# Turned k copied into k's place with a head's rows side by side, and 48 of 64 columns in the k-v product

## The chip, the core and the metric

The kernel runs on one core of a Trainium2 chip, as one launch. The metric is the device time of that launch in microseconds, the median of several runs. The core's engines run side by side: TensorE (PE, matrix products into the PSUM banks; PEld is its loading of weights), VectorE (DVE), ScalarE (ACT), GpSimd (POOL) and SyncE (SP), which issues nearly all DMAs here.

## The reference

A gated linear attention over 768 steps, for 4 batches and 8 heads of 48 columns, and then two dense blocks. In float32 throughout:

```python
for t in range(S):
    state = alpha[:, :, t, :, None] * state + np.einsum('bhd,bhe->bhde', k[:, :, t], v[:, :, t])
    y[:, :, t] = np.einsum('bhd,bhde->bhe', q[:, :, t], state)
x = y.transpose(0, 2, 1, 3).reshape(B * S, H * D)          # 3072 x 384
h = np.maximum(x @ w_in, 0.0); x = h * h @ w_out            # 384 -> 2048 -> 384
h = x @ w_in2;  out = (h / (1.0 + np.exp(-1.702 * h))) @ w_out2
```

## The kernel before

The attention is done in chunks of 64 steps. A step n = 0 to 23 of the kernel handles half of the batches of one chunk (8 pairs of 128 partitions). For each n, `load` brings q, k, decays (tile `raw`, two buffers) and v; `decays`, `ratios`, `carry` prepare them on DVE; `scores`, `state`, `intra` and `gain` are small products on PE; `before`, `causal`, `leave`, `update` move their results on ACT and DVE. `gain(n)` is the k-v product that `update(n)` adds to the state S; it needs k with the steps on the partitions, that is, turned.

The dense blocks work on 512 tokens at a time, with 16 slices j of the hidden width. `inner` (line 182) makes a slice h in one PSUM bank of a rotation of five (`ps`; the banks Y of `scores` and X of `intra` are of the same rotation), ACT takes it out by a relu (L192) and squares it (L197), DVE splits it into a high and a low part (L201, L208), and `outer` (L223) multiplies it on, one or two j later. Every 4 j of the first dense layer form a block m, in which one step of the attention is done as well: `group(m)` holds `scores(m+1)`, `state(m+1)`, `intra(m)`, `gain(m)`, the work on their results, `load(m+2)` and the turning of y and k. In a block with m = 8, 12, 16, 20 the group stands at the fourth j (a late group), in the others at the third. The products of PE in a group other than a late one are followed by the `inner` of the fourth j, in a late one by an `outer`. In the blocks m = 9 to 21 the next layer's weights are also brought in (`w_load`, L79), and made into floats (`w_abs` on ACT, L87, then L96, L99, L102 on DVE). The order of the code is the order on each engine.

For n up to 8, k is turned by PE (`turn`) and copied back into its own place by ACT (`turned`, L432). From n = 9 on, `k_turn` does it without PE: DVE transposes 32 x 32 squares (L455), SP writes them to DRAM in four pieces (L446, tensor `dram_k`), and reads them back turned (L450) into `turned_k`, of which there are two. y goes the same way ahead of k (`y_squares`, L463, `dram_y`), except for m = 11, 15, 19, 23, where PE turns it. The y that came back is split by `x_hi` (L145, ACT) and `x_lo` (DVE) at the second j of the next block.

Of the kernel before, what the change touches and what calls it, by code (L numbers as in the profile page):

```python
# [12 lines left out]
ALU = mybir.AluOpType  # L13
PSUM = bass.MemoryType.PSUM

B, H, S, D = 4, 8, 768, 48
# [3 lines left out]
NHS = (S // CH) * 2  # L20
# [238 lines left out]
def fast(ctx, tc, qka, vs, wpk, out):  # L259
# [8 lines left out]
    nc = tc.nc  # L268
# [45 lines left out]
    def seg(t):  # L314
        return t.rearrange("p (n s) -> p n s", s=SEG)


    st = {}
# [67 lines left out]
    def quarters():  # L386

        for hp in range(4):
            for s in range(2):
                for w in range(2):  # L390
                    yield hp, s, w, 64 * (1 - w)
# [44 lines left out]
    squares = x2[:, 0, NTOK - 512:], x2[:, 1, NTOK - 512:NTOK - 512 + DM]  # L436
    turned_y = x2[:, 2, NTOK - 512:NTOK - 512 + DM]
    turned_k = x2[:, 0:2, NTOK - 1024:NTOK - 512]
# [3 lines left out]
    def shuffle(dst, src, room):  # L442

        w = src.shape[1] // 4
        for i in range(4):
            nc.sync.dma_start(  # L446
                out=room[:, i * w:(i + 1) * w].rearrange("(g p) c -> p g c", g=4),
                in_=src[32 * i:32 * i + 32].rearrange("p (g c) -> p g c", g=4),
            )
        nc.sync.dma_start(out=dst, in_=room)  # L450

    def k_turn(n):
        if n + 2 < NHS:
            k = st[n]["k"]
            nc.vector.transpose(  # L455
                out=squares[0].rearrange("p (g d h) -> p h g d", g=4, h=4),
                in_=k.rearrange("p (h g d) -> p h g d", g=4, h=4),
            )
            shuffle(turned_k[:, n % 2], squares[0], dram_k)
            st[n]["kt"] = turned_k[:, n % 2].rearrange("p (w d h) -> p w h d", w=2, h=4)  # L460

    def y_squares(n):
        nc.vector.transpose(  # L463
# [26 lines left out]
    def gain(n):  # L490

        s = st[n]
        if n + 2 < NHS:
            for hp, b, w, r in quarters():
                h, p = 2 * hp + w, slice(64 * b, 64 * b + 64)
                k = s["kt"][p, 1 - w, hp] if "kt" in s else s["k"][p, hp * 128 + r:hp * 128 + r + 64]
                nc.tensor.matmul(  # L497
                    s["X"][int(r == 64 * b)][r:r + 64, (4 + hp) * D:(5 + hp) * D],
                    lhsT=k, rhs=s["v"][p, h * D:(h + 1) * D],
                    start=True, stop=True,  # L500
                )

# [5 lines left out]
    def heads(t):  # L508
        return t.rearrange("p (h e) -> p h e", e=D)
# [14 lines left out]
    def update(n):  # L524

        if n + 2 < NHS:
            z = S[n % 2].rearrange("p (h b e) -> p h b e", b=2, e=D)
            for b in range(2):
                u = heads(st[n]["X"][1 - b][:, 4 * D:8 * D])
                if n < 2:  # L530
                    nc.scalar.copy(z[:, :, b, :], u)
                else:
                    nc.vector.tensor_tensor(out=z[:, :, b, :], in0=u, in1=z[:, :, b, :], op=ALU.add)

    def sum_up():
        nc.scalar.activation(out=stats, in_=stats, func=AF.Square, accum_out=total)
# [36 lines left out]
    def fill(n):  # L573
        for _ in range(n):
            nc.tensor.matmul(idle_ps, lhsT=idle[:, 0:128], rhs=idle[:, 128:], start=True, stop=True)
# [15 lines left out]
    def pre_split(bi, m):  # L591
# [4 lines left out]
    doing = dict(  # L596
        load_a=load_a, load_q=load_q, decays=decays, ratios=ratios, swap=swap, carry=carry, measure=measure, scores=scores, state=state,
        before=before, causal=causal, turn=turn, turned=turned, intra=intra, gain=gain, leave=leave, update=update,
        y_turn=y_turn, x_hi=x_hi, x_lo=x_lo, k_turn=k_turn, y_squares=y_squares,
    )  # L600

    def do(n, *fs):
        if n < NHS:
            for f in fs:
                doing[f](n)
# [8 lines left out]
    def first_block(what):  # L614
        f, n = what.split(":")
        (doing.get(f) or dense[f])(int(n))

    with tc.manual_schedule():
        nc.vector.memset(idle, 0.0)
        order = ORDER.split()  # L620
        while "load" in order[0]:
            first_block(order.pop(0))
        make_identity(nc, ident)
        nc.gpsimd.memset(mask, 1.0)
        for p0 in (0, 64):
            nc.gpsimd.affine_select(
                out=mask[p0:p0 + 64], in_=mask[p0:p0 + 64], compare_op=ALU.is_ge, fill=0.0, base=0,
                pattern=[[1, CH]], channel_multiplier=-1,
            )
        nc.gpsimd.memset(ones, 1.0)  # L630
        nc.vector.memset(c1, 0)
        nc.vector.memset(seg(c1[:, 1:])[:, :, CH:], 1)
        nc.vector.memset(c2, 0.0)

        nc.scalar.activation(out=total, in_=ones, func=AF.Abs)
        fill(13)
        for what in order:
            first_block(what)
        net.pend.append((0, 0, NJ - 1, net.to_sbuf(x2[:, :, 0:512])))

        def group(m):
            do(m + 1, "scores", "state")
            do(m, "intra", "gain")
            do(m + 1, "before", "causal")
            do(m, "leave", "update")
            if m < NHS - 2:
                load(m + 2)
            if m - 7 < NJ:
                net.w_load(1, m - 7)
            if m % 4 < 3:  # L650
                do(m, "y_squares")
            do(m + 1, "k_turn")

        def turns(m):
            if m % 4 == 3:
                do(m, "y_turn")
            do(m, "x_hi", "x_lo")

        for bi in range(1, NB):
            last = bi == NB - 1  # L660
            between = not last
            for j in range(NJ):
                m, i = 4 * bi + 4 + j // 4, j % 4

                t = 4 * (bi - 1) + j // 4
                if between and i == 2:
                    net.w_bits(1, t)
                net.hidden(0, bi, xs[bi], j)
                if between:
                    if i == 0:  # L670
                        do(m + 1, "decays", "swap")
                        if not t:
                            net.w_load(1, t)
                        if t:
                            net.w_send(1, t - 1, home)
                    elif i == 1:
                        do(m + 1, "ratios", "carry")
                        if j > 1:
                            turns(m - 1)
                        net.w_abs(1, t)  # L680
                    elif i == 2:
                        do(m + 1, "measure")
                    else:
                        net.w_store(1, t, home)

                late = between and j // 4 == 0
                if late and i == 3:
                    group(m)
                if last and j == 0:
                    net.w_send(1, NJ - 1, home)  # L690
                if last and j in (5, 8, 11):
                    pre_split(0, (j - 5) // 3)
                net.pend.append((0, bi, j, net.to_sbuf(x2[:, :, bi * 512:(bi + 1) * 512])))
                if between and j == NJ - 1:
                    net.drain(2)
                    turns(m)
                net.drain(1 if j in (0, NJ - 1) else 2)
                if last and j > 1:
                    net.w_fetch(1, j - 2, home)
                if between and i == 2 and not late:  # L700
                    group(m)
        for bi in range(NB):
            for j in range(NJ):
                net.hidden(1, NB + bi, xs[NB + bi], j)
                if bi + 1 < NB and j in (7, 9, 11):
                    pre_split(bi + 1, (j - 7) // 2)
                if bi == 1 and j == 3:
                    sum_up()

                u = bi * NJ + j - 4  # L710
                c = u // 2
                if u % 2 == 0:
                    if 0 <= c < 2 * NJ:
                        test_load(c)
                    if 0 <= c - 1 < 2 * NJ:
                        test_sum(c - 1)
                elif 0 <= c - 1 < 2 * NJ:
                    test_least(c - 1)
                if bi == 4 and j == 12:
                    counted()  # L720
                if bi == 4 and j == 14:
                    verdict()
                if bi == 5 and j == 4:
                    fine = nc.values_load(flag[0:1, 0:1], min_val=0, max_val=1)
                o = net.to_out(out[bi], x2[:, :, bi * 512:(bi + 1) * 512], bi == NB - 1)
                net.pend.append((1, NB + bi, j, o))
                net.drain(1 if j in (0, NJ - 1) else 2)
                if bi == 0 and j < 2:
                    net.w_fetch(1, NJ - 2 + j, home)
        net.drain(0)  # L730
        return fine
# [159 lines left out]
```

## Time and profile before

| | |
|---|---|
| median of 3 runs | 892.84 us (891.68 to 893.05) |
| the profiled execution, time | 892.36 us |
| its span, first to last instruction | 890.6 us |
| TensorE's granted clock, mean over the span | 0.978 of full |
| busy, PE / DVE / ACT / POOL | 98% / 62% / 48% / 0% of the span |

The profile is of one execution. Its span is what the trace shows; 1.76 us of the measured time lie around it. Matmuls overlap in the pipeline, so how long a group of them takes is read from the start of the group to the start of the next.

### The profile page before, as it was taken

To read this page: it belongs to the slowest core of one execution; us is meant where nothing else is said; L and a number is where in the kernel's file an instruction comes from. 1 tells how busy PE (TensorE), PEld (TensorE's weight loads), DVE (VectorE), ACT (ScalarE), POOL (GpSimd) and SP (SyncE) were. 2 spreads that over 40 slices of the span, in tenths; PEclk is the share of its full clock that TensorE was granted. 3 is DMA by queue.
4 is the path that set the end of the run, shared out by engine and by line. 5 is a ranking of instruction groups with operands and counts; after the bars stand their busy time and mean duration, and the time that the engine had idled before them with its cause. 6 is when DMAs were issued, how large, how long until landed. Compare 5 with 4: busy or idle time off the path is not lost.

```text
span 890.6 us, 15856 instructions
## 1 busy us (share of the span) xinstructions
PE 871.2 (98%) x6487; PEld 718.6 (81%) x6487; DVE 548.1 (62%) x860; ACT 423.3 (48%) x824; POOL 1.4 (0%) x10
## 2 busy tenths in 40 slices
PE   6799999999999999999999999999999999999997
PEld 4688888888888888888888888888888888888885
DVE  8999979768887977975333344444544554433332
ACT  4888764445455444554333343543443444433332
POOL 0000000000000000000000000000000000000000
PEclk6599999999999999999999999999999999999999
DMA  8655216653654655342355423422422432200001
GB/s 330 240 197 177 74 36 198 206 192 121 231 182 141 202 178 189 111 179 90 115 204 182 172 71 107 142 79 99 142 104 74 142 107 71 71 1 4 33 0 40
DMA packets 47009, 116.57 MB, mean 131 GB/s; under 512 B 11216, under 2 KB 22480, under 8 KB 46928
## 3 DMA queue, kind: packets, MB, share of 16 engines
q1 hardware_dynamic: 46784, 115.21, 38.1%
q8 instruction: 53, 0.87, 0.4%
q10 hardware_dynamic: 144, 0.26, 0.1%
q14 instruction: 28, 0.23, 0.1%
HBM read 92.39 MB, written 23.07 MB: 130 GB/s over the span
## 4 chain that ended last, share of the span: by engine, by line
PE 94%; DVE 3%; DMA 1%; issue 1%; ACT 0%; SPq 0%; DVEq 0%
PE h L182 44%; PE acc L223 43%; PE X L497 2%; PE Y L401 2%; PE X L485 1%; PE Y L414 1%; PE kp L427 1%; PE tp L141 0%; DMA x<-qka 0%; DVE raw L341 0%; DMA x<-dram_k 0%; DVE wf L99 0%; DVE M L472 0%; DMA dram_k<-x 0%; DVE y L522 0%
## 5 line engine op out<-in xcount | busy, mean ns | idle before, releaser
L182 PE MATMUL h<-x,w 128*128 128x512 f32 x1728 | 424.7, 391 | 0.0
L182 PEld LDWEIGHTS h<-x,w 128*128 128x128 f32 x1728 | 323.9, 188 | 67.8
L223 PE MATMUL acc<-hi,w 128*128 128x512 f32 x1152 | 298.4, 391 | 0.0
L223 PEld LDWEIGHTS acc<-hi,w 128*128 128x128 f32 x1152 | 214.9, 188 | 44.6
L208 DVE TENSOR_TENSOR lo<-g,hi 128x512 fp32r<-128x512 f32 x192 | 132.9, 692 | 75.3 <-ACT hi L201 67.4
L223 PE MATMUL acc<-lo,w 128*128 128x512 f32 x576 | 165.7, 389 | 0.0
L171 DVE TENSOR_TENSOR g<-h,g 128x512 f32<-128x512 f32 x96 | 66.5, 692 | 152.8 <-ACT g L170 152.8
L170 ACT ACTIVATE g<-h 128x512 f32<-128x512 f32 x96 | 57.5, 599 | 155.8 <-PE h L182 155.4
L192 ACT ACTIVATE g<-h 128x512 f32<-128x512 f32 x96 | 57.4, 598 | 151.4 <-PE h L182 151.0
L223 PEld LDWEIGHTS acc<-lo,w 128*128 128x128 f32 x576 | 108.1, 188 | 22.6
L201 ACT CAST hi<-g 128x512 fp32r<-128x512 f32 x112 | 69.5, 620 | 76.4 <-DVE g L171 76.0
L201 DVE CAST hi<-g 128x512 fp32r<-128x512 f32 x80 | 34.0, 425 | 97.1 <-ACT g L197 97.1
L197 ACT ACTIVATE g<-g 128x512 f32<-128x512 f32 x96 | 60.7, 632 | 2.9
L553 DVE TENSOR_REDUCE ends<-test_f 128x1 f32<-128x768 f32 x32 | 30.3, 948 | 0.0
L549 ACT ACTIVATE test_f<-test 128x768 f32<-128x768 f32 x32 | 29.0, 906 | 0.0
L341 DVE TENSOR_TENSOR_SCAN raw<-raw,c 128x520 f32<-128x520 f32 x20 | 24.7, 1234 | 1.1 <-DMA raw<-qka 1.1
L347 DVE TENSOR_TENSOR_SCAN raw<-raw,c 128x520 f32<-128x520 f32 x20 | 24.9, 1242 | 0.7
L357 DVE TENSOR_TENSOR raw<-raw 128x1024 f32<-128x1024 f32 x20 | 24.4, 1218 | 0.0
L384 ACT ACTIVATE raw<-raw 128x1040 f32<-128x1040 f32 x20 | 21.3, 1065 | 5.5 <-DVE raw L357 5.4
L401 PEld LDWEIGHTS Y<-raw 48*64 48x64 f32 x640 | 12.3, 146 | 11.7 <-issue 6.0
L102 DVE SCALAR_TENSOR_TENSOR wf<-wraw,wf 128x768 int32<-128x768 int32 x22 | 21.1, 958 | 0.8
L99 DVE SCALAR_TENSOR_TENSOR wf<-wraw,wf 128x768 int32<-128x768 int32 x22 | 21.1, 958 | 0.8
(90 smaller groups left out, 513.0 us busy)
## 6 DMA issues: line engine op xcount, KB each, us to landing
test<-wpk SPq DMA_DIRECT2D x32, 768.0 KB, 4.3
wraw<-wpk SPq DMA_DIRECT2D x22, 768.0 KB, 4.7
w<-home SPq DMA_DIRECT2D x16, 768.0 KB, 4.3
raw<-qka SPq DMA_DIRECT2D x20, 512.0 KB, 5.6
x<-wpk SPq DMA_DIRECT2D x10, 768.0 KB, 4.4
home<-whi SPq DMA_DIRECT2D x16, 384.0 KB, 3.6
home<-wf SPq DMA_DIRECT2D x16, 384.0 KB, 4.1
raw<-qka SPq DMA_DIRECT2D x20, 260.5 KB, 4.4
```

The costliest lines, as they stand in the source:

```text
L170: nc.scalar.activation(out=g, in_=h, func=AF.Sigmoid, scale=1.702)
L171: nc.vector.tensor_tensor(out=g, in0=h, in1=g, op=ALU.mult)
L182: self.nc.tensor.matmul(h, lhsT=w[:, a, kk * 128:(kk + 1) * 128], rhs=x[:, b, kk, :], start=(i == 0), stop=(i == 3 * KK - 1),)
L192: self.nc.scalar.activation(out=g, in_=h, func=AF.Relu)
L197: self.nc.scalar.activation(out=g, in_=g, func=AF.Square)
L201: copy(hi, self.h_t[key, j][1])
L208: self.nc.vector.tensor_tensor(out=lo, in0=g, in1=hi.bitcast(F32), op=ALU.subtract)
L223: nc.tensor.matmul(acc[m], lhsT=w[:, a, DM + m * 128:DM + (m + 1) * 128], rhs=g, start=(j == 0 and p == 0), stop=(j == NJ - 1 and p == 2),)
L347: nc.vector.tensor_tensor_scan(out=F, data0=F, data1=c2, initial=0.0, op0=ALU.mult, op1=ALU.add,)
L401: nc.tensor.matmul(s["Y"][w][64 * b:64 * b + 64, hp * CH:(hp + 1) * CH], lhsT=s["k"][r:r + D, c], rhs=s["q"][r:r + D, c], start=True, stop ...
L549: nc.scalar.activation(out=f, in_=high, func=AF.Abs, accum_out=ends[:, c:c + 1])
L553: nc.vector.tensor_reduce(out=ends[:, 2 * NJ + c:2 * NJ + c + 1], in_=tests.pop(c), axis=mybir.AxisListType.X, op=ALU.min)
```

## The change

The squares of k are written with the four heads apart (head, then column) and not interleaved, so that a turned k has 32 columns of a head side by side. A new function `k_place` (line 464 of the new code) copies the turned k on ACT from `turned_k` into the place of k in `raw`, with the 128 values of a head's row in one piece. It is called at the second j of each block, after `ratios` and `carry` of m + 1 and ahead of `turns(m - 1)` (which has `x_hi`, L145) and `w_abs` (L87). `gain` then reads k from `raw` for every n, and for n of 8 and more it loads 48 columns, so that it writes 48 of each 64 rows; `update` therefore works on the two pieces of 48 rows.

```diff
-                out=squares[0].rearrange("p (g d h) -> p h g d", g=4, h=4),
+                out=squares[0].rearrange("p (g h d) -> p h g d", g=4, h=4),
...
-            st[n]["kt"] = turned_k[:, n % 2].rearrange("p (w d h) -> p w h d", w=2, h=4)
+    def k_place(n):
+        if n >= 9 and n + 2 < NHS:
+            nc.scalar.copy(
+                st[n]["k"].rearrange("p (h i d) -> p h i d", h=4, i=4),
+                turned_k[:, n % 2].rearrange("p (i h d) -> p h i d", h=4, i=4),
+            )
...
-                k = s["kt"][p, 1 - w, hp] if "kt" in s else s["k"][p, hp * 128 + r:hp * 128 + r + 64]
+                d = D if n >= 8 else 64
                 nc.tensor.matmul(
-                    s["X"][int(r == 64 * b)][r:r + 64, (4 + hp) * D:(5 + hp) * D],
-                    lhsT=k, rhs=s["v"][p, h * D:(h + 1) * D],
+                    s["X"][int(r == 64 * b)][r:r + d, (4 + hp) * D:(5 + hp) * D],
+                    lhsT=s["k"][p, hp * 128 + r:hp * 128 + r + d], rhs=s["v"][p, h * D:(h + 1) * D],
                     start=True, stop=True,
...
-                else:
-                    nc.vector.tensor_tensor(out=z[:, :, b, :], in0=u, in1=z[:, :, b, :], op=ALU.add)
+                    continue
+                for p in (slice(0, D), slice(64, 64 + D)) if n >= 8 else (slice(0, 128),):
+                    nc.vector.tensor_tensor(out=z[p, :, b, :], in0=u[p], in1=z[p, :, b, :], op=ALU.add)
...
                         do(m + 1, "ratios", "carry")
+                        do(m, "k_place")
                         if j > 1:
                             turns(m - 1)
                         net.w_abs(1, t)
```

On ACT, the second and third j of block 10, before the change: relu and square of the second j, the split of y (L145), the weights' abs (L87), relu and square of the third j, then the sum of magnitudes (L384).

```order
L192 ACTIVATE g_2066<-h_2056 128x512 [waits PE_49]
L197 ACTIVATE g_2066<-g_2066 128x512 [waits Activation_49]
L145 ACTIVATE x_1853,stats_96<-x2_104 128x3x128 [waits DMAHW7_49]
L87 ACTIVATE wf_2077<-wraw_1979 128x768 [waits DMAHW6_49,DMAHW2_49]
L192 ACTIVATE g_2101<-h_2091 128x512 [waits PE_49]
L197 ACTIVATE g_2101<-g_2101 128x512 [waits Activation_49]
```

The same place after the change.

```order
L192 ACTIVATE g_2071<-h_2061 128x512 [waits PE_49]
L197 ACTIVATE g_2071<-g_2071 128x512 [waits Activation_49]
L464 COPY raw_1774<-x2_104 128x512 [waits DMAHW4_49,DMAHW0_49]
L145 ACTIVATE x_1856,stats_96<-x2_104 128x3x128 [waits DMAHW7_49]
L87 ACTIVATE wf_2083<-wraw_1984 128x768 [waits DMAHW6_49,DMAHW2_49]
L192 ACTIVATE g_2107<-h_2097 128x512 [waits PE_49]
L197 ACTIVATE g_2107<-g_2107 128x512 [waits Activation_49]
```

The copy (L464) with its wait for transfers (DMAHW) stands ahead of the split of y, the abs and the relu of the third j.

On SP, the end of block 9's DMAs: the sending of weights (L127, L128), then `load(11)` (L326, L330, L331). Lines with - are before, with + after.

```order
 L127 DMA home<-whi 128x768 [waits Activation_49]
 L128 DMA home<-wf 128x768
-L326 DMA raw<-qka 128x521 [waits DMAHW7_49]
+L326 DMA raw<-qka 128x521 [waits DMAHW7_49,PE_49,Activation_49]
 L330 DMA raw<-qka 128x1024
 L331 DMA v<-vs 128x384
```

The load's first DMA now waits for PE and ACT, which use the k in the buffer that it fills; nothing on SP has changed its place.

On PE, `gain(9)` (L504, L497 before) between the last pass of `intra` and the `inner` of the fourth j (L182), after the change.

```order
L492 MATMUL X_1_1935<-v_1012,M_103 64x48
L504 MATMUL X_0_1934<-v_1012,raw_1011 48x48 [waits Activation_49]
L504 MATMUL X_1_1935<-v_1012,raw_1011 48x48 x2
...
L182 MATMUL h_1998<-x_895,w7_902 128x512 [waits Activation_49]
L182 MATMUL h_1998<-x_895,w7_902 128x512 x8
```

`gain` reads `raw` and waits for ACT (before: `x2`, and for DMAs); the `inner` behind it waits for ACT, as it did before, since its bank is that of the slice five banks earlier in the rotation (h of the third j, then two Y and two X).

## Rows read from the trace of the kernel before

**Rows 1.** Page, parts 1 (busy us, share, instructions) and 4 (chain that ended last).

```profile
PE 871.2 (98%) x6487; PEld 718.6 (81%) x6487; DVE 548.1 (62%) x860; ACT 423.3 (48%) x824; POOL 1.4 (0%) x10
...
PE 94%; DVE 3%; DMA 1%; issue 1%; ACT 0%; SPq 0%; DVEq 0%
```

**Rows 2.** Busy time by window: length, PE, PEld, DVE, ACT, POOL, clock, DMA.

```profile
135.60:390.00 254.40, 254.05 (x2636) 211.46 (x2632) 206.46 (x349) 121.26 (x244) 0.00 (x0) 1.00 0.56 183
```

**Rows 3.** PE by time: start, us, line, output<-inputs, count [idle before <-releaser].

```profile
135.02 0.64 PE L497 MATMUL X<-v,raw 64*64 64x48 f32 x32
135.59 1.66 PE L223 MATMUL acc<-hi,w 128*128 128x512 f32 x6
...
152.07 1.18 PE L497 MATMUL X<-v,x 64*64 64x48 f32 x32 [0.35 <-DMA x<-dram_k]
153.17 2.32 PE L182 MATMUL h<-x,w 128*128 128x512 f32 x9
...
170.67 0.65 PE L485 MATMUL X<-v,M 64*64 64x48 f32 x32
171.14 1.13 PE L497 MATMUL X<-v,x 64*64 64x48 f32 x32
172.20 2.36 PE L182 MATMUL h<-x,w 128*128 128x512 f32 x9
...
191.27 2.36 PE L182 MATMUL h<-x,w 128*128 128x512 f32 x9
...
212.74 1.66 PE L223 MATMUL acc<-hi,w 128*128 128x512 f32 x6
...
229.77 2.36 PE L182 MATMUL h<-x,w 128*128 128x512 f32 x9
```

**Rows 4.** DVE by time, block 10: first weights line, `update`, k's squares.

```profile
168.28 0.55 DVE L96 TENSOR_SCALAR wf<-wf 128x768 int32<-128x768 int32 x1
...
173.06 0.61 DVE L533 TENSOR_TENSOR S<-X,S 128x192 f32<-128x192 f32 x2
173.59 0.57 DVE L463 STREAM_TRANSPOSE x<-y 128x384 f32<-128x384 f32 x1
174.08 1.06 DVE L455 STREAM_TRANSPOSE x<-raw 128x512 f32<-128x512 f32 x1
```

**Rows 5.** Groups by line: the copy of `turned`; busy us, mean ns | idle.

```profile
L432 ACT COPY raw<-kp 128x512 f32<-128x512 f32 x5 | 2.9, 586 | 2.8 <-PE kp L427 1.8 <-PE Y L401 1.0
```

**Rows 6.** SP's DMA issues by time, groups 8 and 10.

```profile
135.81 0.33 SPq L326 DMA_DIRECT2D raw<-qka  x1
...
140.43 1.78 SPq L446 DMA_DIRECT2D dram_y<-x  x4
145.29 0.34 SPq L450 DMA_DIRECT2D x<-dram_y  x1
...
148.97 0.34 SPq L450 DMA_DIRECT2D x<-dram_k  x1
...
166.20 0.60 SPq L326 DMA_DIRECT2D raw<-qka  x1
...
174.19 1.75 SPq L446 DMA_DIRECT2D dram_y<-x  x4
177.31 0.34 SPq L450 DMA_DIRECT2D x<-dram_y  x1
```

**Rows 7.** Page, part 6: DMA, count, KB each, median us from issue to landing.

```profile
x<-dram_k SPq DMA_DIRECT2D x13, 256.0 KB, 3.0
```

**Rows 8.** ACT by time, second and third j of block 9.

```profile
144.79 0.63 ACT L197 ACTIVATE g<-g 128x512 f32<-128x512 f32 x1
147.69 0.53 ACT L145 ACTIVATE x<-x 128x384 fp32r<-128x384 f32 x1 [2.27 <-DMA x<-dram_y]
...
148.22 0.88 ACT L87 ACTIVATE wf<-wraw 128x768 f32<-128x768 f32 x1
149.01 0.57 ACT L192 ACTIVATE g<-h 128x512 f32<-128x512 f32 x1
```

More of the change, by code (lines that the diff above doesn't have):

```diff
@@ L598, in fast @@
         before=before, causal=causal, turn=turn, turned=turned, intra=intra, gain=gain, leave=leave, update=update,
-        y_turn=y_turn, x_hi=x_hi, x_lo=x_lo, k_turn=k_turn, y_squares=y_squares,
+        y_turn=y_turn, x_hi=x_hi, x_lo=x_lo, k_turn=k_turn, k_place=k_place, y_squares=y_squares,
     )
```

## Prediction

> **What bounds the kernel now.** I read the page first: TensorE (PE) is busy 98% of the span and carries 94% of the chain that ended last [rows 1]. Then the busy times of three stretches: between 135.6 and 390 us, where every instruction of the change lies, PE is busy 254.05 of 254.40 us at full clock, and VectorE (DVE) 206, ScalarE (ACT) 121 [rows 2]. So here PE never has a gap to give away: a microsecond taken out of its instructions shortens the kernel, and a microsecond that it waits lengthens it, with no later slack in which to recover. Two questions decide: what `gain` costs PE, and whether anything that moved makes PE wait.
>
> **What is removed.** In PE's order of time, `gain(8)`, which still reads contiguous rows, runs from 135.02 to the next line's 135.59: 0.57 us for 32 passes. `gain(10)`, which reads every fourth word, runs from 171.14 to 172.20: 1.06 us. `intra`, 32 passes of the same size with contiguous weights, takes 0.47 (170.67 to 171.14) [rows 3]. After the change a `gain` should lie between 0.47 and 0.57; I take 0.54, nearest to the row of the same product, so 0.52 less, 13 times (n = 9 to 21): 6.8 us. `gain(9)` also loses its 0.35 us wait for the turned k [rows 3]. The 48 columns have no row of their own; whether they save more is bounded by those same two values, and `gain(8)` gets at most 0.1.
>
> The Trainium skill's "TensorE: Matmul & The Clock Gate", section "LDWEIGHTS (loading the stationary operand)", says that a weight load costs time in proportion to its columns. By that 48 of 64 columns would take the 0.47 to an estimated 0.35, and the sum below would be about 0.5 us lower, since most blocks turn out to be limited elsewhere; no row here shows a 48-column load.
>
> **What is added and is hidden.** The square transposes of k now write contiguously; today they take 1.06 us each, and the writes that follow them on SP wait for the y squares' read anyhow, so they end early either way [rows 4]. Their transfers keep their sizes. `update` has four instructions where it had two: two cost 0.53 us of DVE (173.06 to 173.59) [rows 4]. With half of the partitions one could cost half as much or the same; I take the same, +0.53. The copy on ACT has the size of `turned`'s, 586 ns from PSUM [rows 5]; next start after 0.57.
>
> **What is moved.** Two waits are new, and both sit ahead of other work. First, `load(m+2)` reuses the buffer whose k `gain(m)` now reads, so SP holds it until PE has done `gain(m)`. Today it goes out before: 166.20 for `gain(10)` at 171.14 [rows 3, 6]. Behind it on SP stand the weights' load, the y squares and the k squares. Only `gain(8)` waits like this today, since it reads k in place: there the load starts at 135.81, 0.22 us after `gain(8)`, the y writes at 140.43, and because these lie behind the loads the y read starts 4.86 us later (145.29), against 3.12 us (174.19 to 177.31) where the load went out earlier. The k read starts 3.68 us after it (148.97) and takes 3.0 [rows 6, 7]; PE's start at 152.07 after a wait for it agrees [rows 3]. So turned k arrives 16.4 us after such a `gain`.
>
> Second, ACT executes in order, and `k_place` stands at the second j of a block, ahead of the x copy (L145), the weights' abs (L87) and the next j's relu (L192). ACT is free there at about 145.4, so `k_place(9)` waits some 6.5 us. Then come copy 0.57 and, from the start of L145 to the end of that relu, 1.89 us (147.69 to 149.58) [rows 8]. That relu frees the PSUM bank that the product after `gain` needs. So PE's next `inner` starts no earlier than 16.4 + 0.57 + 1.89 = 18.9 us after the last `gain`'s end.
>
> **The sum, block by block** (m has four j; counted at the start of the `inner` after `gain`).
> *Blocks 13, 17, 21*, after a `gain` late in its block, and block 9: before, 17.03 us (212.74 to 229.77), and 17.58 for block 9 (135.59 to 153.17) [rows 3]. `gain(12)`, `gain(16)` and `gain(20)` now have the load pattern of `gain(8)`, so all take 18.9: +1.9 three times, +1.3 once.
> *Blocks 10, 11, 14, 15, 18, 19*: PE alone needs 19.07 (172.20 to 191.27) [rows 3] less 0.52, 18.55. Against it stands a loop: the abs is finished 0.5 us before the relu ends (149.10, 149.58) [rows 8]; from the following L96 to the y writes 5.91 (168.28 to 174.19) [rows 4, 6] plus 0.53 for `update`, so 6.0 after the relu; y read 3.12 later, k read 3.68, landing 3.0, copy and relu 2.46: 18.26. The loads delay the y writes by between 0 and 1.74 us (4.86 less 3.12). In the first of each pair the load starts 7 us ahead of the y writes, near the 8 of the undisturbed case (166.20 to 174.19): +0.2, so 18.5, no stall (`gain(9)` ends at 17.0 + 0.54, its load goes out at 17.8, the y writes at 18.9 + 6.0). In the second it starts 5.7 ahead (37.7 to 43.4); a y read 9.48 after the load, as at n = 8 (135.81 to 145.29), gives +0.6, 18.9. So the pair saves 0.5 and 0.2.
> *Blocks 12, 16, 20*: no y squares stand before the k squares, the loop loses over 3.5 us and doesn't bind; the full 0.52 is saved.
> Sum: 4 late blocks 3 × 1.87 + 1.32 = +6.9; three pairs -2.1; three others -1.6: +3.2 us. On the profiled execution's own 892.36 this is 895.6; on the median, 892.84, it is 896.0. I put down 895.8.
>
> **The rivals.** A difference below 0.2% (1.8 us) can't be told from no change here.
> *The loads cost the turned k nothing* (other side, faster): the place is the y writes of blocks after a late `gain`. If they take 3.12 us instead of 4.86, and go out 4.84 us after `gain` as at n = 8, the `inner` starts 4.84 + 3.12 + 3.68 + 3.0 + 2.46 = 17.1 after it, or 17.6 with `update`'s 0.53; that is about as before (+1.7 to -0.3 in all four), and the nine other blocks keep 0.52 each, -4.7: together -3 to -5, 888.4. It decides where the arrival of k falls 1.2 us or more below 16.4. For it: in the later late blocks the weights' load could land sooner, and no row shows them behind a held load. Against: n = 8 shows the pattern itself.
> *The wait is free*: if PE doesn't need that relu, or the copy waits nowhere, all 13 savings stay, -7.1 us, 885.3. Against it: ACT's order puts the copy first, and the transfer is seen to land after ACT is free.
> *The loop binds*: if the loads cost every block 1.74 us, the loop is 20.0, each of the six blocks loses 0.9, and the end is some +11, 903; half of that delay gives +6, 898.5.
> *Half-way*: late blocks stall about 1 us less, the rest as above: within 0.2%.
>
> **How the numbers follow.** Likeliest (893.6 to 898): 0.43. Loop binds: 0.12. Half-way: 0.17. Loads free: 0.22. Wait free: 0.06. That is slower 0.55, same 0.17, faster 0.28. The bounds on single costs (`gain` 0.47 to 0.57, `update` 0 to 0.53, the copy a few tenths) move each case by about 1 us. The range of 8 in 10 leaves out the free wait and the upper half of the binding loop: 887.5 to 900.
>
> **What would show it.** In the profile after: `gain` at 0.5 us; `load(m+2)` starting 0.2 us after `gain(m)`; ACT's copy waiting 4 to 7 us for the turned k in most blocks; PE waiting for ACT at the `inner` after `gain(9)`, `gain(13)`, `gain(17)`, `gain(21)`, 1 to 2.5 us each, and hardly elsewhere. Wrong would be: no wait at those four, a load not held back, or a copy far from 0.6 us.

## The result, and the profile after

The changed kernel takes 903.4 us in the median (899.98 to 905.73, four runs), the kernel before 892.94 beside it (891.68 to 894.12, four runs): a ratio of 1.0114 [1.0078, 1.015]. It became 10.5 us slower. The prediction had the sign, 895.8 us, but not the size; the time lies outside its range.

The profiled execution of the changed kernel is the fastest of the four, 899.98 us with a span of 898.2; before, the span was 890.6. So the trace shows 7.6 us of the loss. The page's busy times (first line) and its chain by engine, which answer to [rows 1]:

```profile
PE 865.9 (96%) x6487; PEld 710.5 (79%) x6487; DVE 556.0 (62%) x888; ACT 427.7 (48%) x837; POOL 1.4 (0%) x10
...
PE 77%; DVE 8%; DMA 7%; issue 3%; SPq 2%; ACT 2%; DVEq 0%; ACTq 0%
```

PE's share of the chain fell from 94% to 77%; most of what it lost went to DVE (3% to 8%) and DMA (1% to 7%). The windows, with the columns of [rows 2], the long stretch first and then three microseconds twice, show how much PE lost there:

```profile
135.60:390.00 254.40, 243.63 (x2609) 199.04 (x2600) 206.22 (x360) 121.06 (x247) 0.00 (x0) 0.99 0.55 175
152.00:155.00 3.00, 0.79 (x33) 0.67 (x34) 1.24 (x3) 2.64 (x6) 0.00 (x0) 0.92 0.60 212
155.00:158.00 3.00, 3.00 (x8) 2.33 (x9) 2.83 (x5) 1.87 (x5) 0.00 (x0) 0.52 0.73 205
```

PE had 0.35 us idle in the long stretch before and has 10.8 now. And the granted clock, 1.00 in the long stretch before, is 0.52 in the stretch from 155 to 158, near the lower of its two levels (1.2 of 2.4 GHz), just after PE had done 0.79 us of work in the 3 us before. What PE waited for, of the changed kernel (us in total, times, longest), between 135.6 and 395 us:

```profile
PE h L182 <- ACT g L192: 6.2, 6, 1.2
PE X L504 <- ACT raw L464: 2.5, 3, 1.2
PE h L182 <- DVE x L149: 1.7, 3, 0.6
PE tp L141 <- DVE y L529: 0.8, 3, 0.3
```

The first line is the wait that was forecast, for the relu behind the copy. The second is for the copy itself. The last two, in blocks 12, 16 and 20, stood in no part of the forecast. PE by time, changed kernel, columns as in [rows 3]:

```profile
153.00 0.57 PE L504 MATMUL X<-v,raw 64*48 64x48 f32 x32 [1.24 <-ACT raw L464]
154.79 3.77 PE L182 MATMUL h<-x,w 128*128 128x512 f32 x9 [1.21 <-ACT g L192]
158.39 1.54 PE L223 MATMUL acc<-hi,w 128*128 128x512 f32 x6
...
174.22 0.56 PE L504 MATMUL X<-v,raw 64*48 64x48 f32 x32
174.71 1.66 PE L182 MATMUL h<-x,w 128*128 128x512 f32 x6
...
193.49 2.34 PE L182 MATMUL h<-x,w 128*128 128x512 f32 x9 [0.24 <-ACT g L192]
...
198.14 0.52 PE L141 MATMUL tp<-ident,y 128*128 128x128 f32 x3 [0.27 <-DVE y L529]
...
202.65 0.97 PE L182 MATMUL h<-x,w 128*128 128x512 f32 x3 [0.56 <-DVE x L149]
...
215.19 0.56 PE L504 MATMUL X<-v,raw 64*48 64x48 f32 x32
215.68 0.50 PE L223 MATMUL acc<-hi,w 128*128 128x512 f32 x1
...
233.74 2.35 PE L182 MATMUL h<-x,w 128*128 128x512 f32 x9 [1.21 <-ACT g L192]
```

`gain` takes 0.49 us (174.22 to 174.71) where it took 1.06: that gain is there in full. `gain(9)` waits for the copy, and the `inner` behind it waits again, for the relu. That `inner` then takes 3.60 us (154.79 to 158.39), where before it took 2.16, from 153.17 [rows 3] to the line behind it:

```profile
155.33 1.52 PE L223 MATMUL acc<-hi,w 128*128 128x512 f32 x6
```

So the low clock costs 1.44 us on the spot. Note also that a stop costs PE more than its listed idle time: from `gain(9)` to the `inner` are 1.79 us, not 0.49, so 1.30 for a listed 1.21.

ACT by time at the second and third j of block 11, and the copy of block 13:

```profile
190.98 0.62 ACT L464 COPY raw<-x 128x512 f32<-128x512 f32 x1 [4.41 <-DMA x<-dram_k]
191.51 0.52 ACT L145 ACTIVATE x<-x 128x384 fp32r<-128x384 f32 x1
...
192.03 0.94 ACT L87 ACTIVATE wf<-wraw 128x768 f32<-128x768 f32 x1
192.87 0.57 ACT L192 ACTIVATE g<-h 128x512 f32<-128x512 f32 x1
...
231.28 0.62 ACT L464 COPY raw<-x 128x512 f32<-128x512 f32 x1 [5.17 <-DMA x<-dram_k]
```

In the trace of before the same L145 of block 11 waited for nothing:

```profile
183.99 0.51 ACT L145 ACTIVATE x<-x 128x384 fp32r<-128x384 f32 x1
```

It now starts 7.52 us later, because it stands behind a copy that waits for the turned k. DVE at the same place, changed kernel:

```profile
192.15 0.56 DVE L149 TENSOR_TENSOR x<-x,x 128x384 fp32r<-128x384 f32 x1 [2.72 <-ACT x L145]
193.00 0.56 DVE L96 TENSOR_SCALAR wf<-wf 128x768 int32<-128x768 int32 x1 [0.29 <-ACT wf L87]
...
197.38 0.61 DVE L529 TENSOR_TENSOR y<-X,y 128x192 f32<-128x192 f32 x2
197.91 1.45 DVE L542 TENSOR_TENSOR S<-X,S 48x192 f32<-48x192 f32 x4
199.40 0.71 DVE L455 STREAM_TRANSPOSE x<-raw 128x512 f32<-128x512 f32 x1
...
202.04 0.56 DVE L149 TENSOR_TENSOR x<-tp,x 128x384 fp32r<-128x384 f32 x1
```

DVE idles 2.72 us for ACT's split and then works without a gap from 193.00 to the x split at 202.04, which PE waits for. The four instructions of `update` take 1.49 us (197.91 to 199.40) where the two took 0.53 [rows 4]; the k squares take 0.71 instead of 1.06. Last, SP after `gain(12)`, which ends at 215.68:

```profile
215.88 0.33 SPq L326 DMA_DIRECT2D raw<-qka  x1
...
221.55 1.75 SPq L446 DMA_DIRECT2D dram_y<-x  x4
224.59 0.34 SPq L450 DMA_DIRECT2D x<-dram_y  x1
...
228.31 0.34 SPq L450 DMA_DIRECT2D x<-dram_k  x1
```

The load starts 0.20 us after `gain`, as forecast. The y writes go out 5.87 us after `gain`, the y read 3.04 later, the k read 3.72 later, and the copy starts 2.97 after that: 15.60 us. With 2.46 from copy to `inner` (231.28 to 233.74) that is the 18.06 which block 13 takes.

**Where the 7.6 us are.** Counted as in the prediction, from the start of the product behind one `gain` to the start of the product behind the next, after less before: late blocks 9, 13, 17, 21: +1.57, +1.03, +1.86, +1.15, together +5.6. Blocks 10, 11, 14, 15, 18, 19: -0.2 in all, 1.44 for the clock included. Blocks 12, 16, 20: +0.72, +0.75, +0.69, together +2.2. The sum is the difference of the spans.

The other three runs have spans of 901.0, 902.3 and 903.9 us at mean granted clocks of 0.976, 0.975 and 0.973, against 0.979 in the profiled one. A mean lower by 0.006 over 900 us is 5.4 us of full clock; the slowest run is 5.7 longer. But that mean also holds the first 46 us of the launch, whose own clock differs from trace to trace (0.59 in that of before, 0.67 in that of the changed kernel), and that alone makes 0.004 of the mean. So what the median adds to the trace can't be put down to the clock by these means; e11 below has a trace of a longer run.

### The profile page after: what moved, and what is told of

It is laid out like the page before. It is cut to its first block, busy times and chain, and to the rows that moved or that the text cites. A ratio compares the mean times of both kernels' runs of the same rounds, so it can differ in the third digit from the quotient of the medians.

```text
span 898.2 us, 15895 instructions
## 1 busy us (share of the span) xinstructions
PE 865.9 (96%) x6487; PEld 710.5 (79%) x6487; DVE 556.0 (62%) x888; ACT 427.7 (48%) x837; POOL 1.4 (0%) x10
## 4 chain that ended last, share of the span: by engine, by line
PE 77%; DVE 8%; DMA 7%; issue 3%; SPq 2%; ACT 2%; DVEq 0%; ACTq 0%
PE h L182 37%; PE acc L223 36%; DMA x<-dram_k 3%; SPq L446 2%; DMA dram_k<-x 2%; DVE S L542 1%; DMA raw<-qka 1%; PE Y L401 1%; PE X L492 1%; DVE wf L122 1%; DMA dram_y<-x 1%; PE X L504 1%; PE Y L414 1%; DVE wf L99 1%; DVE M L479 1%
## 5 line engine op out<-in xcount | busy, mean ns | idle before, releaser
L182 PE MATMUL h<-x,w 128*128 128x512 f32 x1728 | 426.7, 393 | 8.0 <-ACT g L192 6.2
L182 PEld LDWEIGHTS h<-x,w 128*128 128x128 f32 x1728 | 324.6, 189 | 77.7 <-ACT g L192 7.4
L464 ACT COPY raw<-x 128x512 f32<-128x512 f32 x13 | 8.0, 616 | 43.2 <-DMA x<-dram_k 43.2
L364 ACT COPY r<-raw 64x8 f32<-64x8 f32 x18 | 3.7, 204 | 44.0 <-DVE raw L341 44.0
L542 DVE TENSOR_TENSOR S<-X,S 48x192 f32<-48x192 f32 (+1 forms) x68 | 23.4, 352 | 1.0 <-PE X L504 0.4
L384 ACT ACTIVATE raw<-raw 128x1040 f32<-128x1040 f32 x20 | 21.2, 1062 | 4.5 <-DVE raw L357 4.4
```

Of the source, the lines that this page charges most:

```text
L182: self.nc.tensor.matmul(h, lhsT=w[:, a, kk * 128:(kk + 1) * 128], rhs=x[:, b, kk, :], start=(i == 0), stop=(i == 3 * KK - 1),)
L542: nc.vector.tensor_tensor(out=z[p, :, b, :], in0=u[p], in1=z[p, :, b, :], op=ALU.add)
```

## The experiments

All times are medians in us; before beside them on the same chip was 892.74 to 892.98. "Steps" are the 13 stretches between the products behind two `gain`s, counted as above, blocks 9 to 21, which sum to 247.4 before and 255.1 after.

| kernel | copy stands | place of k | `update` | us (lowest to highest, runs) | ratio |
|---|---|---|---|---|---|
| changed | second j, ahead of split and abs | `raw` | 4 pieces | 903.4 (899.98 to 905.73, 4) | 1.0114 [1.0078, 1.015] |
| e2 | the same | own | 4 pieces | 901.22 (900.42 to 903.03, 4) | 1.0105 [1.009, 1.0121] |
| e4 | the same | `raw` | whole | 899.63 (896.67 to 904.92, 6) | 1.0086 [1.0057, 1.0115] |
| e10 | the same | own | whole | 891.25 (888.46 to 893.07, 12) | 0.9979 [0.9969, 0.9989] |
| e9 | second j, behind split and abs | `raw` | 4 pieces | 889.2 (887.12 to 892.31, 8) | 0.9962 [0.9948, 0.9976] |
| e3 | third j | `raw` | 4 pieces | 889.39 (888.13 to 892.28, 10) | 0.9969 [0.9958, 0.998] |
| e7 | third j | `raw` | whole | 889.07 (887.87 to 892.78, 12) | 0.9966 [0.9954, 0.9978] |
| e8 | third j | own | whole | 887.0 (885.99 to 888.4, 5) | 0.9939 [0.9925, 0.9952] |
| e1 | no copy | k's read sorts | whole | 910.36 (908.44 to 913.59, 5) | 1.0204 [1.0185, 1.0223] |
| e5 | none, load held | before's | whole | 896.04 (893.59 to 900.25, 7) | 1.0037 [1.0019, 1.0056] |
| e6 | as changed, `gain` thrice | `raw` | 4 pieces | 904.8 (902.38 to 905.83, 5) | 1.013 [1.0112, 1.0147] |

The theory after the result: a copy that waits on ACT ahead of other work closes a loop, which `update` and the held load make longer. The rivals: the held load alone, `update` alone, or the clock alone. No kernel leaves out a part of the computation; e5 and e6 add products.

**e1: the same weight layout, but without a copy on ACT.** The kernel before, with the sorting done by the DMAs: the squares are written in pieces of 128 bytes, and the read brings whole rows, from which `gain` takes its 64 columns in one piece.

```diff
-            shuffle(turned_k[:, n % 2], squares[0], dram_k)
+            room = dram_k.rearrange("(p g) (h i d) -> p (g h) i d", g=4, h=4, i=4)
+            for i in range(4):
+                nc.sync.dma_start(
+                    out=room[:, :, i], in_=squares[0][32 * i:32 * i + 32].rearrange("p (x d) -> p x d", d=32),
+                )
+            nc.sync.dma_start(out=turned_k[:, n % 2], in_=dram_k.rearrange("(p g) c -> g p c", g=4))
```

> The kernel before, but the four DMA writes of the k squares go out in pieces of 32 columns, so that the turned k arrives with a head's 64 values side by side and gain reads it where it lands: no copy on ScalarE, no read of raw, update whole, 64 columns. First theory (the weight layout is worth 0.5 us a gain; the loss comes from the copy's place on ScalarE and from the load that it holds back): 885.5 to 888, with gain at 0.5 us and no wait for ScalarE. Rival (the layout costs elsewhere: the writes of small pieces land later and PE waits at gain in the blocks after a late group): 889 to 893. If the loss came from DVE's extra update instructions or the layout itself, nothing would be gained: 893 or more.

It took 910.36 us, and the theory was missed; it is far beyond the rival's 889 to 893 too, though the rival named the reason: the transfers, not ACT, became the wait. PE's row at `gain(9)`:

```profile
157.39 1.10 PE L502 MATMUL X<-v,x 64*64 64x48 f32 x32 [5.82 <-DMA x<-dram_k]
158.43 3.62 PE L182 MATMUL h<-x,w 128*128 128x512 f32 x9
```

SP had issued this k read at 149.96 us, so it took about 7.4 us to `gain`, where [rows 7] has 3.0. PE waits 16.1 us in four such places (blocks 9, 13, 17, 21), and in or just behind each the granted clock falls to half: the `gain` here takes 1.04 us. The blocks without a wait take 18.56 and 20.97 us, 0.5 less than before, so the layout itself is not what costs, and its gain doesn't need the copy; but by this way it costs 17.4 us.

**e2: the copy goes to a place of its own,** so that `load(m+2)` need not wait for `gain(m)`.

```diff
+            kc = x2[:, 2, NTOK - 1024:NTOK - 512]
             nc.scalar.copy(
-                st[n]["k"].rearrange("p (h i d) -> p h i d", h=4, i=4),
+                kc.rearrange("p (h i d) -> p h i d", h=4, i=4),
...
+            st[n]["k"] = kc
```

> The changed kernel, with the copy going to a place of its own (a free part of x2) and not into raw, so that load(m+2) isn't held back until gain(m). The copy stays where it is on ScalarE. First theory (a held load makes the turned k land some 2.4 us later, and ScalarE waits for it ahead of its other work): turned k lands about 14 us after a late gain, ScalarE's wait shrinks from 4 to 6 us to 1 to 4, PE hardly waits: 888 to 892. Rival (the copy's place alone is enough, the load doesn't matter): 898 or more. Rival (DVE's four update instructions): unchanged, 900 to 905.

It took 901.22 us, not the first theory's 888 to 892, and PE waits for the same things as in the changed kernel (6.8 us for the relu, 2.7 for the copy, 1.7 and 0.8 for DVE). The held load isn't the cause by itself.

**e3: the copy at the third j.** One line is moved, from the second j to the third, behind `measure`; split and abs no longer stand behind it.

```diff
                         do(m + 1, "ratios", "carry")
-                        do(m, "k_place")
                         if j > 1:
                             turns(m - 1)
                         net.w_abs(1, t)
                     elif i == 2:
                         do(m + 1, "measure")
+                        do(m, "k_place")
```

> The changed kernel, with the copy one j later on ScalarE: behind the split of y, the weights' abs and the third j's relu and square, directly ahead of the group. The load stays held. First theory: only gain itself can wait for the copy, by about 1 us in the four blocks after a late group; relu, split and DVE's work are on time again: 888 to 892, PE's waits at the inner after gain gone. Rival (the held load is what costs): still 898 or more, with PE waiting at gain instead. Rival (DVE's update): 900 to 905.

It took 889.39 us: 14 us less than the changed kernel by one moved line, and less than before. PE waits in this stretch only at `gain`, for the copy, in blocks 9, 13, 17 and 21 (us in total, times, longest), never for a relu and never for DVE:

```profile
PE X L504 <- ACT raw L464: 3.5, 4, 1.3
```

Blocks 12, 16 and 20 take 20.87, 0.60 less than before.

**e9: the copy at the second j, but behind the turns and the abs.** This tells the split's delay from that of the third j's relu, which still stands behind the copy.

```diff
                         do(m + 1, "ratios", "carry")
-                        do(m, "k_place")
                         if j > 1:
                             turns(m - 1)
                         net.w_abs(1, t)
+                        do(m, "k_place")
```

> The changed kernel with the copy moved by two instructions on ScalarE: still at the second j and ahead of the third j's relu, but behind the split of y and the weights' abs. Update split, load held. First theory (the copy delays the split and the abs, these DVE's weight bits, update and the y squares, and these the next turned k: a loop of about 18.5 to 20 us): the loop is cut, only the relu behind the copy is late, by up to 1 us in the blocks after a late group: 888 to 891. Rival (the relu, whose bank the next inner needs, is what PE waits for, wherever the abs stands): 896 to 902.

It took 889.2 us, within the theory's 888 to 891. Its ACT at the place of block 11 that was shown above:

```profile
187.39 0.62 ACT L464 COPY raw<-x 128x512 f32<-128x512 f32 x1 [2.63 <-DMA x<-dram_k]
187.92 0.59 ACT L192 ACTIVATE g<-h 128x512 f32<-128x512 f32 x1
```

The copy still waits (2.63 us, since ACT comes to it later; 4.41 in the changed kernel), and it starts no earlier: 16.28 us after `gain(10)`, against 16.27 in the changed kernel. But only the copy's own 0.53 us lies between that wait and the relu, not 1.89 with split and abs, and these two started at 12.23 and 12.76 us after `gain(10)`, near their 11.79 and 12.30 of before. What is left of PE's waits is again for the copy itself, at `gain` in blocks 9, 13, 17 and 21, and not for the relu, where the theory had it:

```profile
PE X L504 <- ACT raw L464: 3.3, 4, 1.1
```

So the copy's own wait costs about as much as in e3; the rest of the loss came from the split and the abs that stood behind it.

**e5: only the held load.** The kernel before, with one small product added from block 9 on that reads the k in `raw` behind `gain`; nothing uses its result.

```diff
+            if n >= 9:
+                nc.tensor.matmul(
+                    s["X"][0][0:D, 8 * D:8 * D + 64], lhsT=s["k"][64:64 + D, 0:D], rhs=s["k"][64:64 + D, 0:64],
```

> The kernel before with the load held alone: after gain(m), for m of 9 and more, one small product reads k in raw, so that load(m+2) waits for it; its result is used by nothing. First theory: the turned k lands about 2.4 us later in the blocks after a late group, where PE had 1.9 us to spare at gain: waits of about 0.4 us there, 893 to 895. Rival (the held load is what costs the changed kernel its time): 898 or more.

It took 896.04 us, 3.1 more than before, between the theory's range and the rival's. The steps of its trace grow by 3.2, of which the added product itself is about 1.0 (blocks 12, 16, 20, which wait for nothing, take 21.56 instead of 21.47, so 0.08 thirteen times). Of the rest, block 21 (+1.2) and block 9 (+0.4) have a `gain` that waits for the k, 0.89 and 0.64 us (before: not at all and 0.35); in block 14 (+0.7) the added product starts 0.46 us late, for no release that the trace shows. The k read of blocks 13, 17 and 21 goes out 0.9, 1.2 and 3.2 us later after `gain` than before, and only in the last does PE feel it. So the held load alone is far from the whole loss.

**e4: only `update` whole.** The changed kernel with 64 columns in `gain` and two instructions in `update`.

```diff
-                d = D if n >= 8 else 64
+                d = 64
...
-                for p in (slice(0, D), slice(64, 64 + D)) if n >= 8 else (slice(0, 128),):
+                for p in (slice(0, 128),):
```

> The changed kernel with 64 columns in gain and update whole, two DVE instructions of 128 partitions and not four of 48; the copy stays at the second j. In the traces the four take 1.49 us from the first's start to the next instruction (two took 0.53), 0.96 more, ahead of the y squares on DVE. Theory (the copy's place makes a loop from the turned k over ScalarE and DVE back to the squares, and update's 0.96 us lengthen that loop): a shorter loop, stalls smaller in every block but 9, 895 to 899. Rival (update's instructions are the whole loss): 885 to 889. Rival (they are hidden): 900 to 905 as in the changed kernel.

It took 899.63 us, just above the theory's 895 to 899. The waits of 0.6 us for DVE in blocks 12, 16 and 20 are gone (21.30, 20.97 and 21.31 us against 22.2), but those for the relu did not become smaller as the theory had it: 6.8 us in all, 6.2 in the changed kernel. One of them, at block 17:

```profile
307.44 0.68 PE L504 MATMUL X<-v,raw 64*64 64x48 f32 x32 [0.68 <-ACT raw L464]
309.24 3.50 PE L182 MATMUL h<-x,w 128*128 128x512 f32 x9 [1.11 <-ACT g L192]
```

Again two stops, and an `inner` of 3.30 us behind them (to 312.54) in place of 2.16.

**e6: `gain` done three times in blocks 9, 13, 17, 21,** to keep PE at work over the late relu; the repeated products give the same values.

```diff
+            times = 3 if n in (9, 13, 17, 21) else 1
-            for hp, b, w, r in quarters():
+            for hp, b, w, r in [x for _ in range(times) for x in quarters()]:
```

> The changed kernel, with the products of gain done three times over in blocks 9, 13, 17 and 21 (the same values written again): 1 us more work for PE in the four places where it then waits 1.2 us for ScalarE at the next inner. Theory (where PE stands still for over 2 us the granted clock falls to half for some 3 us, at 1.5 us each, in a number of blocks that differs from run to run): the stall is filled, no fall, all runs within 1 us of 898 to 899 and the trace at full clock after gain(9). Rival (the spread of 900 to 906 has another cause): runs as before, 900 to 906, up to 1 us more.

It took 904.8 us, and the expectation was missed. In its trace the clock of the stretch from 135.6 to 390 is 1.00, and block 10 takes 19.15 where it took 19.92; but the late blocks became longer (19.46, 19.64, 20.21 in 9, 13, 17). What the clock costs in the median it doesn't tell.

**e7 and e8: third j and `update` whole, with the held load and without.** The edits of e3 and e4, for e8 that of e2 as well.

> The copy at the third j, ahead of the group, and update whole with 64 columns; the load still held. Theory: DVE's 0.96 us lie on the way to the k that gain(13), gain(17), gain(21) wait for (0.5 us each with the copy at the third j), so these waits go: 887 to 889. Rival (DVE's time is hidden here): 888 to 892, as with the copy at the third j alone.

> The same, and the copy goes to a place of its own, so that the load isn't held. Theory: the only wait left is that of gain(9), behind the load that gain(8) holds back anyway: 885.5 to 888, 0.5 to 0.8% faster than before. Rival (the earlier load costs the transfers as much as it gives): 888 to 890.

e7 took 889.07 us, like e3: with the copy out of the loop, 48 columns with four pieces and 64 with two come out alike. The waits at `gain` became less than in e3 but did not go, as the theory had it (0.28, 0.75 and 0.34 us in blocks 13, 17 and 21, against 0.49, 0.52 and 1.23). e8 took 887.0, the fastest of all, 5.7 us below before. PE by time in e8, at `gain(9)` and `gain(10)`:

```profile
153.19 0.68 PE L506 MATMUL X<-v,x 64*64 64x48 f32 x32 [0.95 <-ACT x L465]
...
171.79 0.65 PE L506 MATMUL X<-v,x 64*64 64x48 f32 x32
172.37 2.34 PE L182 MATMUL h<-x,w 128*128 128x512 f32 x9
```

The first is its only wait in the stretch. `gain` with 64 contiguous columns takes 0.58 us (171.79 to 172.37), with 48 it took 0.49.

**e10: only the place.** The copy as in the changed kernel, ahead of the split; own place and whole `update`.

> The changed kernel with update whole (64 columns) and the copy to a place of its own (load not held), the copy at its place at the second j, ahead of the split: beside the version with the copy at the third j (887.0) it differs in the place alone. First theory: the place alone keeps most of the loss, waits of 0.5 to 1.2 us at the inner after most gains: 896 to 900. Rival (the place hurts only together with the held load or the split update): 887 to 891.

It took 891.25 us where the theory had 896 to 900 and the rival 887 to 891: the place alone costs about 4 us against e8, and the rest of the loss comes only where the place meets the held load or the pieces of `update`. PE waits 3.4 us for relus in five places and 0.7 for the copy, and at block 9:

```profile
152.37 0.68 PE L506 MATMUL X<-v,x 64*64 64x48 f32 x32 [0.74 <-ACT x L465]
154.16 3.91 PE L182 MATMUL h<-x,w 128*128 128x512 f32 x9 [1.11 <-ACT g L192]
```

**e11: the changed kernel as it is, once more,** for a second trace of the same program.

> The changed kernel again, one look, for the clock. Theory (the granted clock falls to half after some of the double waits of over 2 us, at 1.5 us each): the sum of PE's waits as in the first trace, within 1 us, and the span follows the number of falls that the windows show: 898 with one, 901 with three, 904 with five. Rival: the spans differ by waits of PE, with the clock the same.

It took 906.18 us, with a span of 904.4, and its waits are not the first trace's: up to 396 us they sum to 15.7 us against 11.2. The steps sum to 258.1 against 255.1, and another 3.3 us lie behind block 21. That the waits repeat within a microsecond was wrong, and so was the span for one fall of the clock (898). PE at the end of block 21, and then windows as above:

```profile
391.82 0.57 PE L504 MATMUL X<-v,raw 64*48 64x48 f32 x32 [2.16 <-ACT raw L464]
393.61 4.21 PE L182 MATMUL h<-x,w 128*128 128x512 f32 x9 [1.22 <-ACT g L192]
```

```profile
394.00:397.00 3.00, 3.00 (x8) 2.32 (x8) 2.83 (x5) 1.70 (x5) 0.00 (x0) 0.50 0.76 230
397.00:400.00 3.00, 3.00 (x9) 2.34 (x9) 2.93 (x9) 1.95 (x3) 0.00 (x0) 0.59 0.93 323
400.00:403.00 3.00, 3.00 (x15) 2.47 (x14) 1.95 (x4) 0.21 (x1) 0.00 (x0) 1.00 0.32 84
```

Here the clock is low for about 7 us behind two stops, which costs 2.7 us (from this `inner` to the next, at 400.54, are 6.93 us, in the first trace 4.21); at block 9, where the same trace has stops of 1.32 and 1.21 us, it did not fall. So of the 6.2 us between the two traces 4.5 are listed waits, and the clock makes some 1.3 (2.7 here, 1.44 there).

## Why the prediction was wrong

Against the forecast of +3.2 us the trace has +7.6. By the forecast's own terms, the late blocks came out 1.3 us better than put down, the three pairs 1.9 worse, and blocks 12, 16 and 20 3.8 worse; the other runs, and so the median, lie up to 5.7 further on.

**What was right.** The gain of the layout: 0.54 was forecast for `gain`, 0.49 came, and where nothing waits a block saves 0.5 to 0.6 (e3, e8, e9). The Trainium skill's "TensorE: Matmul & The Clock Gate", section "LDWEIGHTS (loading the stationary operand)", has load time go with the columns. By that 48 of 64 would take e8's 0.58 to an estimated 0.44; the trace shows 0.49, so the direction agrees and the size is smaller. The held load (0.20 us after `gain`) and PE's waits for ACT in the late blocks were right too: "all take 18.9" came out at 19.15, 18.06, 18.89 and 18.17. The copy waits in ten of 13 places, but 4 us or more, as put down for most, in only five of them.

**The step that failed:** "Blocks 12, 16, 20: no y squares stand before the k squares, the loop loses over 3.5 us and doesn't bind; the full 0.52 is saved." The k did come in time: the copy waits in 10 of 13 places, and not in these three. But I looked at k alone. In the block ahead of each, the copy holds the split and the abs back, so DVE gets to its weights late and stays behind: `update(11)` starts 4.42 us after the `inner` behind `gain(11)`, in the trace of before 0.85 (191.27 to 192.12). In just these blocks PE turns the y itself, and it waits for DVE to finish that y (0.27 us) and to split it (0.56). Put down were -1.6 us; it became +2.2. With the copy behind split and abs (e9) these waits are gone and the blocks take 20.87, which is 0.60 saved where 0.52 was forecast. They are gone as well with the copy ahead and `update` whole (e4, e10), and not with the load free alone (e2): it took the place and the four pieces together.

**`update`:** "With half of the partitions one could cost half as much or the same; I take the same, +0.53." It was +0.96. That decides in the loop. Here is one block of a pair, block 15, read from the timelines of PE, SP and ACT; all in us after the start of the product behind `gain(14)`:

| kernel | split | y writes | y read | k read | copy | next `inner` |
|---|---|---|---|---|---|---|
| before | 11.79 | 1.99 | 6.06 | 9.73 | none | 19.07 |
| changed | 16.68 | 6.50 | 9.53 | 13.23 | 16.15 | 18.65 |
| e2, own place | 16.78 | 6.50 | 9.53 | 13.23 | 16.25 | 18.76 |
| e10, own place, `update` whole | 15.79 | 5.41 | 8.44 | 12.13 | 15.27 | 18.56 |
| e9, copy behind the abs | 11.78 | 3.99 | 9.17 | 12.85 | 15.89 | 18.48 |
| e8, third j, own place, whole | 11.77 | 2.46 | 6.36 | 10.03 | 16.83 | 18.56 |

With the copy ahead of the split, the split of one block sets the y writes of the next, and these set the k and so the next split. The loop's length is the copy's start and 2.46 us to the `inner`: 16.15 + 2.46 = 18.61 in the changed kernel, where 18.26 was forecast; `update` alone is 0.43 more than put down. PE alone needs 18.48 (block 15 in e9 and e3). In e10 it is 17.73, and there PE has 0.8 us to spare. Where the k takes longer than usual this is not enough: block 14 of e10 has its copy at 16.89 and takes 19.37. In e9 and e8 the split no longer hangs on the k, and the loop is open.

**"So the pair saves 0.5 and 0.2"** came out at 0.2 for all three pairs together in place of 2.1. Of the 1.9 in between, 1.44 is the clock in block 10; in block 14 PE waits 1.07 us for the relu behind a late copy, and it takes 19.63; the other four take 18.5 to 18.8 and together save 0.5 more than was put down. The rival "the loop binds" named 903, which is what the median shows, but not by its way: it had six blocks lose 0.9 each, and four of them save 0.3 to 0.5.

**The late blocks: right in size, by another way.** I had the held load obstruct the y writes, 4.86 us to the read in place of 3.12. In block 13 the read follows after 3.04; what is late is the start of the writes, 5.87 us after `gain(12)` with `update` in pieces, 4.83 with it whole (e8, and e7 with the load held). The obstruction exists: in e4, held load and `update` whole, blocks 13, 17 and 21 have the read 4.33, 4.59 and 5.36 after writes at 4.83. So the pieces and the held load cover each other in part, and taking away one alone (e2, e4) gives back only 2 to 4 us of the 14 that the place is worth.

**No term for the clock.** The forecast counted a wait as the time waited. In the traces of the changed kernel, e2, e4 (twice), e10 and e11, two stops of PE behind one another were followed by a stretch at about half clock, and the `inner` behind them took 3.30 to 4.01 us, 1.1 to 1.9 more than 2.16. In all, the low clock cost 1.44 us in the trace of the changed kernel and 2.7 in e11. What makes the other runs longer than the traced one is not shown by their mean clocks; in e11, the only longer run with a trace, it was waits for the greater part.

**What stays open.** Which stops bring the clock down: 1.24 and 1.21 us did at block 9, 1.32 and 1.21 at the same place in e11 did not, a single stop of 1.30 in e3 did not, and the single stops of 3.1 to 5.8 us in e1 all did. Why the waits of one program differ between runs. And how much of the 903.4 of the median, against the 899.98 that was traced, is waits and how much is clock.

## What to carry to other kernels

Before an instruction that waits for a transfer is put on an in-order engine, list everything behind it on that engine up to the next wait, and follow each of these to its own consumers: here one line moved behind a split and an abs turned 10 us lost into 4 us won. If that work feeds the next transfer of the kind that is waited for, it is a loop: compare its length with the bounding engine's time, and when the two are within a microsecond, costs on other engines stop being free. On an engine that bounds the kernel, count a stop as more than its idle time.

## What the runs showed that was not expected

- An addition on 48 partitions is not cheaper on DVE than one on 128: four took 1.49 us, two whole ones 0.53, so even 0.37 for one against 0.27.
- With the k round trip written in pieces of 128 bytes (e1), 6.7 to 7.4 us passed from the read's issue to the `gain` that waited for it, in four blocks, against 3.1 at `gain(9)` before, for the same bytes. Whether the pieces or the read's new order of rows did that is not told apart.
- Two stops of PE with only a `gain` between them, 0.7 to 2.2 us long, were followed by half clock for some microseconds, but not always; the `inner` behind them took 3.30 to 4.01 us in place of 2.16.
- A stop costs PE 0.1 us or so more than the idle time that the trace lists.
